# Transposing the attention output and the normalised rows of the last two chunks by DMA from SBUF instead of TensorE

## The chip, the cores and the metric

The kernel runs on one core of a Trainium2 chip. The metric is device microseconds of one execution, lower is better. Engines are named as in the profile: PE (TensorE), PEld (its weight loads), DVE (VectorE), ACT (ScalarE), POOL (GpSimd) and SP, the sync engine, whose queue issues all the DMAs of the part studied here (160 to 330 us), one after the other in program order. The record sorts runs into fast and slow ones; all runs quoted were in the fast state.

## The reference

It computes one transformer block forward and all its gradients, for 2048 tokens of width 640 in bfloat16: pre-norm linear attention (32 heads of width 20), then a gated MLP with 1728 hidden units. Only the forward pass between attention and MLP matters here.

```python
o = num / den                                   # linear attention, per head
h = x + o.reshape(B, S, D) @ wo                 # projection of the attention output
hn = layernorm(h)                               # "normalised rows"
gate, up = hn @ w1, hn @ w3                     # MLP, first matmuls
h2 = h + (silu(gate) * up) @ w2
```

In this kernel's matmuls the dimension that is summed over lies on the partitions, so `o` and `hn`, which are made with tokens on partitions, are transposed before `@ wo` and `@ w1`. Its PE transposes end in PSUM, where its matmul results go, and ScalarE copies them to SBUF (0.69 to 0.72 us for the five of a tile in the stretch used below).

## The kernel before

The 2048 tokens are four chunks of 512, each of four tiles of 128 tokens. While the MLP of chunk c runs in 14 steps (`fc`), the attention output, projection and norm of chunk c+1 are squeezed in between as "side" work. Position 0 lies between the gate and the up matmuls of a step, position 1 behind the step. Cuts are marked with `...`.

```python
def f2_o(t):                                   # DVE: attention output of tile t
    ...
    dma(out=o_v[:, t, :], in_=o_t[:])          # store, needed by the backward pass
    oT[t] = o_t

def f2_ot(t):                                  # PE transposes + ACT copy
    tr = ps.tile([P, DT, P], BF16, name="tr", bufs=1)
    for c in range(DT):                        # DT = 5 blocks of 128x128
        T.transpose(tr[:, c, :], oT[t][:, c * P:(c + 1) * P], ident[:])
    oT[t] = pf.tile([P, DT, P], BF16, name="oT", bufs=2)
    A.copy(out=oT[t][:], in_=tr[:])

def f2_at(t, tag="nd"):                        # projection with wo, PE waits for oT
    ...
def f2_hn(t):                                  # DVE: normalised rows, then their store
    ...
def f2_ht(t):                                  # the same five transposes for hn -> hnT
    ...

for i in range(TPC):                           # TPC = 4 tiles; (step, position, what)
    for k, pos, f in ((3 * i, 0, f2_ndo), (3 * i + 1, 1, f2_ot), (3 * i + 2, 1, f2_at), (3 * i + 3, 0, f2_hn),
                      (3 * i + 4, 0, f2_ht)):
        side[pos].setdefault(k, []).append((f, i))
```

Each MLP step also ends with three stores on SP (`hh_d`, and `gg_d` twice), which wait for DVE (one `hh_d` goes out at 231.57 us, DVE having finished its `hhT` at 231.54).

Of the kernel before, what the change touches and what calls it, by code (L numbers as in the profile page):

```python
# [8 lines left out]
P = 128  # L9
# [16 lines left out]
HD = D // 2  # L26
NG = 27
NB, NBLK = 288, 6


def _heads(lo, hi, g):
# [31 lines left out]
def kernel(  # L63
# [280 lines left out]
        oT[t] = o_t  # L344

    def f2_ot(t):
        tr = ps.tile([P, DT, P], BF16, name="tr", bufs=1)
        for c in range(DT):
            T.transpose(tr[:, c, :], oT[t][:, c * P:(c + 1) * P], ident[:])
        oT[t] = pf.tile([P, DT, P], BF16, name="oT", bufs=2)  # L350
        A.copy(out=oT[t][:], in_=tr[:])
# [36 lines left out]
    def f2_ht(t):  # L388
        c, i = divmod(t, TPC)
        if i == 0:  # L390
            hnT[c] = pf.tile([P, DT, W], BF16, name="hnT", bufs=2)
        tr = ps.tile([P, DT, P], BF16, name="tr", bufs=1)
        for d in range(DT):
            T.transpose(tr[:, d, :], hn[t][:, d * P:(d + 1) * P], ident[:])
        A.copy(out=hnT[c][:, :, i * P:(i + 1) * P], in_=tr[:])  # L395
# [81 lines left out]
    w2 = U1.tile([P, FT, D], BF16, name="w2", tag="D")  # L477
    V.memset(w2[64:, FT - 1, :], 0.0)

    side = ({}, {})  # L480
    for i in range(TPC):
        for k, pos, f in ((3 * i, 0, f2_ndo), (3 * i + 1, 1, f2_ot), (3 * i + 2, 1, f2_at), (3 * i + 3, 0, f2_hn),
                          (3 * i + 4, 0, f2_ht)):
            side[pos].setdefault(k, []).append((f, i))

    for c in range(SC):
        hhT[c] = pa.tile([P, FT, W], BF16, name="hhT", bufs=2)
        o2 = o2_steps(c - 1) if c > 0 else None

        def run_side(pos, fc):  # L490
            if c + 1 < SC:
                for f, i in sorted(side[pos].get(fc, ()), key=lambda x: x[1]):
                    f((c + 1) * TPC + i)

        for fc in range(FT):
            mlp(c, fc, lambda: run_side(0, fc))
            if o2:
                next(o2)
            run_side(1, fc)
            if fc == 1 and c == 0:  # L500
                dma(out=w2[:, 0:FT - 1, :], in_=B_w2[0:(FT - 1) * P, :].rearrange("(c p) n -> p c n", p=P))
                dma(out=w2[0:FL, FT - 1, :], in_=B_w2[(FT - 1) * P:F, :])
            if fc == 3 and c + 1 < SC:
                load_g2T(c + 1)
            if c == SC - 1 and fc == 0:
                g2 = U1.tile([P, ST, D], BF16, name="g2", tag="Q")
                for i in range(SC):
                    dma(out=g2[:, i * TPC:(i + 1) * TPC, :], in_=goS[:, i * TPC:(i + 1) * TPC, :])
            if c == SC - 1 and fc == 4:
                woT = U1.tile([P, DT, D], BF16, name="woT", tag="W6")  # L510
                dmaT(out=woT[:], in_=A_wo[:, :])
# [75 lines left out]
    def h1b(n):  # L587
        return ps.tile([P, n, P], BF16, name="h1b", tag="h1", bufs=2)
# [63 lines left out]
    def b_ln(acc, t):  # L652
        ln_rest[t] = ln_bwd(acc, t, hnb[t][:], ln2, g_h[:, t, :], g2[:, t, :], br)

    def b_gT(t):
        tr = h1b(DT)
        for c in range(DT):
            T.transpose(tr[:, c, :], g_h[:, t, c * P:(c + 1) * P], ident[:])
        ghT[t] = br.tile([P, DT, P], BF16, name="ghT", bufs=2)
        A.copy(out=ghT[t][:], in_=tr[:])  # L660
# [5 lines left out]
    def b_go(t):  # L666
        gnd[t] = gnd_s[t % 2]
        gv = gnd[t][:, 0:C].rearrange("p (h e) -> p h e", e=DA)
        prod = br.tile([P, H, DH], BF16, name="prod")
        gd = br.tile([P, H], F32, name="gd", bufs=2)  # L670
        for j in range(2):
            go = h1()
            hs = slice(j * 16, (j + 1) * 16)
            for c in range(DT):
                T.matmul(go[:, 0:HD], lhsT=ghT[t][:, c, :], rhs=woT[:, c, j * HD:(j + 1) * HD], start=(c == 0),  # L675
                         stop=(c == DT - 1))
            V.tensor_tensor(out=gv[:, hs, 0:DH], in0=go[:, 0:HD].rearrange("p (h d) -> p h d", d=DH),
                            in1=rden[:, t, hs].unsqueeze(2).to_broadcast([P, 16, DH]), op=ALU.mult)
        V.tensor_tensor(out=prod[:], in0=gv[:, :, 0:DH], in1=o_sb[:, t, :].rearrange("p (h d) -> p h d", d=DH),
                        op=ALU.mult)  # L680
        V.reduce_sum(out=gd[:], in_=prod[:], axis=AX.X)
        V.tensor_scalar(out=gv[:, :, DH], in0=gd[:], scalar1=-1.0, scalar2=None, op0=ALU.mult)

    def b_gndT(t):
        tr = h1b(CT)
        for cc in range(CT):
            T.transpose(tr[:, cc, :], gnd[t][:, cc * P:(cc + 1) * P], ident[:])  # L687
        gndT[t] = br.tile([P, CT, P], BF16, name="gndT", bufs=2)
        A.copy(out=gndT[t][:], in_=tr[:])

    def b_gkv(t):
        for m, (a, b) in enumerate(M_H):
            bank, off = KV_SLOT[m]
            T.matmul(gkv[:, bank, off:off + M_W[m]], lhsT=pqb[t][:, m * P:(m + 1) * P],
                     rhs=gnd[t][:, a * DA:b * DA], start=(t == 0 and off == 0), stop=(t == ST - 1),
                     skip_group_check=True)
# [33 lines left out]
    for t in range(ST + 3):  # L730
        g = b_ghn(t) if t < ST else wog

        def part():
            next(g, None)

        u, w = t - 2, t - 3
        if t + 2 < ST:
            b_load(t + 2)
        if 0 <= t - 1 < ST:
            b_load_q(t - 1)  # L740
        if t % 2 == 0 and 2 <= t <= ST - 2 and t // 2 + 1 < ST // 2:
            load_gg(t // 2 + 1)
        if 0 <= u < ST:
            b_gT(u)
        if t == ST:
            ln_rest.pop(t - 1)()
        part()
        if w >= 0:
            b_gndT(w)
            b_gkv(w)  # L750
        part()
        if 0 <= u < ST:
            b_go(u)
        part()
        if t - 1 in ln_rest and t < ST:
            ln_rest.pop(t - 1)()
        part()
        if w >= 0:
            b_gpq(w)
        part()  # L760
        part()
        if t == ST:
            xnN = U1.tile([P, ST, D], BF16, name="xnN", tag="Q")
            for i in range(SC):
                dma(out=xnN[:, i * TPC:(i + 1) * TPC, :], in_=xS[:, i * TPC:(i + 1) * TPC, :])
        if t > ST:
            for i in range(8):
                j = (t - ST - 1) * 8 + i
                ln1.norm(xnN[:, j, :], xnN[:, j, :], j)
# [100 lines left out]
    def load_block(i):  # L870
        if i < len(blocks):
            base, _, f0 = blocks[i]
            gb[i] = ex.tile([P, ST, NB], BF16, name="gb", bufs=3)
            dmaT(out=gb[i][:], in_=gg_d[base + f0:base + f0 + NB, :])

    for i in range(SC):
        dma(out=hnN[:, i * TPC:(i + 1) * TPC, :], in_=hn_v[:, i * TPC:(i + 1) * TPC, :])
    load_block(0)
    load_block(1)
    gT = {}  # L880

    def e_T(t, k):
        if k == 0:
            gT[t] = ex.tile([P, 15, P], BF16, name="gT", bufs=2)
        tr = ps.tile([P, DT, P], BF16, name="trq", bufs=2)
        for c in range(DT):
            T.transpose(tr[:, c, :], gqkv[k][:, t, c * P:(c + 1) * P], ident[:])  # L887
        if k == 1:
            V.tensor_copy(out=gT[t][:, k * DT:(k + 1) * DT, :], in_=tr[:])
        else:  # L890
            A.copy(out=gT[t][:, k * DT:(k + 1) * DT, :], in_=tr[:])

    def e_gxn(t):
        acc = ps.tile([P, 2, 512], F32, name="gxn", tag="gxn", bufs=2)
        for j in range(2):
            for k in range(15):
                T.matmul(acc[:, j, 0:HD], lhsT=gT[t][:, k, :], rhs=wqT[:, k, j * HD:(j + 1) * HD],  # L897
                         start=(k == 0), stop=(k == 14))
                if j * 15 + k in (7, 15, 23) and t + 1 < ST:
                    e_T(t + 1, (j * 15 + k) // 8)  # L900
        gx = ex.tile([P, D], BF16, name="gx", bufs=2)
        ln_bwd(acc, t, xnN[:, t, :], ln1, gx[:], g_h[:, t, :], ex)()
        A.dma_start(out=out1S[:, t, :], in_=gx[:])
# [5 lines left out]
    for k in range(3):  # L909
        next(jobs)  # L910
        next(jobs)
        e_T(0, k)
    for t in range(ST):
        next(jobs, None)
        e_gxn(t)
    for _ in jobs:
        pass

# [2 lines left out]
    ps = pool("pfp", space=PSUM)  # L921
    njob = 8
    for i, (_, out, f0) in enumerate(blocks):
        load_block(i + 2)
        for m in range(DT):
            grad_job(hnN, m, lambda t: gb[i][:, t, :], NB, out[:, m, f0:f0 + NB])
    ps.release()
# [35 lines left out]
```

## Time and profile before

| | before |
|---|---|
| time, median of 3 | 919.74 us (919.29 to 919.98) |
| PE busy | 96% of the span |
| PE busy, 165 to 305 us | 139.2 of 140 us |
| DVE, ACT busy, same stretch | 114.6 and 85.8 us |

How to read it: PE is busy 99% of this stretch and the list of its waits is empty there, so I take PE as what sets the pace. The lines themselves stand in the prediction below.

To compare kernels I use one **stretch**: from the start of the first group of output matmuls (`o<-w,hhT`) that runs between the MLP steps of chunk 1 to the first that runs between those of chunk 3. It holds all sixteen groups of transposes that the change removes. In the kernel before, its two ends are these lines of PE's timeline (start, duration, engine, line, operation, out<-in, shapes, count):

```profile
168.34 1.25 PE L448 MATMUL o<-w,hhT 128*128 128x320 bf16 x8
...
307.58 1.25 PE L448 MATMUL o<-w,hhT 128*128 128x320 bf16 x8
```

307.58 - 168.34 = 139.24 us. (The expectations for the first eight runs count the stretch from and to other marks, which makes it 135.99 us before.)

### The profile page before, as it was taken

Reading aid. Unit: us, or ns where it says so; the run is one execution under the profiler, and the core shown is the slowest. Engines: PE = TensorE matmul, PEld = TensorE weight load, DVE = VectorE, ACT = ScalarE, POOL = GpSimd, SP = SyncE. Lnnn points to the kernel's source line nnn. Section 1 sums busy time; section 2 is a strip of 40 time slices with the busy share of each in tenths; the row PEclk is TensorE's granted clock in tenths of the full one; section 3 lists DMA queues with packets and bytes.
Section 4 is the critical chain, followed back from the end, with each engine's and each line's share of the span. In section 5 each row is a group of like instructions: output and inputs, shape, how many; then the busy total and the mean of one; then the engine's idle time right before and its main releaser. Section 6 shows DMA issues by size and latency. Waiting matters only on the chain.

```text
span 917.3 us, 16861 instructions
## 1 busy us (share of the span) xinstructions
PE 883.4 (96%) x6729; PEld 611.5 (67%) x6757; DVE 449.0 (49%) x1146; ACT 388.7 (42%) x722; POOL 22.5 (2%) x42
## 2 busy tenths in 40 slices
PE   5999899999999999899999999999899999999998
PEld 3777554555555555677677777777677777777776
DVE  6776688888888677200145655555323443400000
ACT  3556777665565665011123223223334545422211
POOL 4000000000000000000000000000000000000000
PEclk9999999999999999999999999999999999999999
DMA  9678583353343552999444555148996011066861
GB/s 297 188 246 258 147 240 119 99 141 108 99 136 115 176 168 93 230 224 265 133 134 125 153 163 144 37 165 174 219 275 153 33 40 38 28 153 150 178 149 37
DMA packets 272447, 138.33 MB, mean 151 GB/s; under 512 B 173808, under 2 KB 271088, under 8 KB 272368
## 3 DMA queue, kind: packets, MB, share of 16 engines
q1 hardware_dynamic: 253856, 124.05, 51.8%
q10 hardware_dynamic: 18512, 13.20, 4.6%
q8 instruction: 53, 0.87, 0.4%
q14 instruction: 26, 0.21, 0.1%
HBM read 45.20 MB, written 50.02 MB: 104 GB/s over the span
## 4 chain that ended last, share of the span: by engine, by line
PE 82%; DVE 2%; DMA 2%; ACT 2%; issue 1%; ACTq 0%; DVEq 0%
PE job L796 20%; PE mm L400 19%; PE ghn L625 13%; PE gxn L897 7%; PE gw L559 7%; PE o L448 5%; PE h L675 2%; PE at L361 2%; PE gwo L716 2%; DMA hb<-hh_d 2%; PE trq L887 1%; DMA vaT<-va_d 1%; PE dkv L702 1%; PE h L702 1%; PE h1b L687 1%
## 5 line engine op out<-in xcount | busy, mean ns | idle before, releaser
L400 PE MATMUL mm<-hnT,w 128*128 128x512 bf16 x546 | 132.7, 379 | 1.7 <-ACT hnT L395 1.0
L796 PE MATMUL job<-gb,hnN 128*128 128x288 bf16 x960 | 117.8, 286 | 0.0
L796 PEld LDWEIGHTS <-hnN 128*128 128x128 bf16 x960 | 93.9, 98 | 23.7
L625 PEld LDWEIGHTS <-ggb 128*128 128x128 bf16 x864 | 82.4, 98 | 30.2 <-issue 0.5
L400 PEld LDWEIGHTS <-w 128*128 128x128 bf16 x560 | 53.8, 98 | 61.3 <-issue 1.1
L800 ACT CAST obs<-job 128x288 bf16<-128x288 f32 (+1 forms) x90 | 36.8, 409 | 132.9 <-PE job L796 88.0
L897 PE MATMUL gxn<-wqT,gT 128*128 128x320 bf16 x480 | 74.8, 299 | 0.0
L400 PE MATMUL mm<-g2T,w2T 128*128 128x512 bf16 x266 | 68.3, 379 | 0.8
L448 PE MATMUL o<-w,hhT 128*128 128x320 bf16 x448 | 67.9, 299 | 1.0 <-DVE h L453 1.0
L625 PE MATMUL ghn<-w13a,ggb 128*128 128x320 bf16 x448 | 67.8, 299 | 0.0
L559 PE MATMUL gw<-g,hb 128*128 128x320 bf16 (+1 forms) x448 | 61.1, 299 | 1.3 <-DMA hb<-hh_d 1.3
L219 PE MATMUL big<-wqkv,pqT 128*128 128x320 bf16 x400 | 59.6, 305 | 2.7 <-DVE kvacc L258 1.0
L625 PE MATMUL ghn<-w13b,ggb 128*128 128x320 bf16 x416 | 61.2, 299 | 0.0
L448 PEld LDWEIGHTS <-hhT 128*128 128x128 bf16 x448 | 43.8, 98 | 24.9 <-issue 1.2
L219 PEld LDWEIGHTS <-pqT 128*128 128x128 bf16 x480 | 46.4, 99 | 20.8 <-DVE kvacc L258 1.3
L412 ACT CAST ghh<-mm 128x512 bf16<-128x512 f32 x56 | 32.9, 588 | 63.3 <-issue 39.3
L796 PEld LDWEIGHTS <-xnN 128*128 128x128 bf16 x480 | 47.2, 99 | 18.5
L559 PEld LDWEIGHTS <-hb 128*128 128x128 bf16 (+1 forms) x448 | 44.1, 99 | 18.4 <-DMA hb<-hh_d 1.7
L897 PEld LDWEIGHTS <-gT 128*128 128x128 bf16 x480 | 45.1, 98 | 14.8
L636 ACT ACTIVATE gs<-ghn 128x640 bf16<-128x640 f32 x16 | 11.3, 705 | 95.8 <-PE ghn L625 95.8
L648 ACT ACTIVATE y<-wb,s,ln_rs 128x640 bf16<-128x640 f32 x32 | 29.4, 920 | 40.9 <-DVE wb L644 40.9
L420 ACT ACTIVATE sig<-mm 128x512 bf16<-128x512 f32 x56 | 33.4, 597 | 24.8 <-PE mm L400 24.1
(136 smaller groups left out, 1212.0 us busy)
## 6 DMA issues: line engine op xcount, KB each, us to landing
ggb<-gg_d SPq DMA_DIRECT2D x8, 1728.0 KB, 9.5
hh_d<-hhT SPq DMA_DIRECT2D x52, 128.0 KB, 1.8
gg_d<-gate SPq DMA_DIRECT2D x52, 128.0 KB, 1.9
gg_d<-sig SPq DMA_DIRECT2D x52, 128.0 KB, 1.8
out_dram<-obs ACTq DMA_DIRECT2D x60, 72.0 KB, 2.7
w<-in_B_w_dram SPq DMA_DIRECT2D x4, 864.0 KB, 5.5
va_d<-va SPq DMA_DIRECT2D x4, 768.0 KB, 6.5
out_dram<-gw2o ACTq DMA_DIRECT2D x18, 160.0 KB, 4.7
```

What stands on the lines that cost most here:

```text
L219: T.matmul(acc, lhsT=pqT[:, c, t * P:(t + 1) * P], rhs=wqkv[:, c, n0:n0 + HD], start=(c == 0), stop=(c == DT - 1))
L361: T.matmul(at[:, 0:HD], lhsT=oT[t][:, c, :], rhs=wo[:, c, j * HD:(j + 1) * HD], start=(c == 0 and not on_pe), stop=(c == DT - 1))
L400: T.matmul(acc[:], lhsT=w[:, c, fc * P:(fc + 1) * P], rhs=rhs[:, c, :], start=(c == 0), stop=(c == DT - 1))
L412: A.copy(out=ghh[fc][:], in_=acc[:])
L420: A.activation(sig[:], gp[:], AF.Sigmoid)
L448: T.matmul(o2["ps"][:, 0:HD], lhsT=hhT[c][:, fc, i * P:(i + 1) * P], rhs=w2[:, fc, j * HD:(j + 1) * HD], start=(fc == 0), stop=(fc == FT - 1))
L559: T.matmul(acc[:n, j, 0:HD], lhsT=hb[b][:, t, i * P:i * P + n], rhs=g2[:, t, j * HD:(j + 1) * HD], start=(t == 0), stop=(t == ST - 1))
L625: T.matmul(acc[:, j, 0:HD], lhsT=ggb[t // 2][:, k, lo:lo + P], rhs=rhs[:, j * HD:(j + 1) * HD], start=(k == 0), stop=(k == NG - 1))
L648: A.activation(out=y[:], in_=wb[:], func=AF.Identity, bias=s[:, 3:4], scale=st.rs[:, t:t + 1])
L796: T.matmul(acc[:, 0:n], lhsT=lhs[:, t, m * P:(m + 1) * P], rhs=rhs(t), start=(t == 0), stop=(t == ST - 1))
L800: A.copy(out=ob, in_=acc[:, 0:n])
L897: T.matmul(acc[:, j, 0:HD], lhsT=gT[t][:, k, :], rhs=wqT[:, k, j * HD:(j + 1) * HD], start=(k == 0), stop=(k == 14))
```

## The change

Its intent is to take work off PE, the bound: the transposes of chunks 2 and 3 (tiles 8 to 15) become DMA transposes, SBUF to SBUF, on the SP queue, and the ACT copies out of PSUM vanish. As a DMA takes time to land (2.6 us in the median here, see below), the attention output's transpose is moved one step earlier, to just behind the step that makes it, and that of the normalised rows from inside a step to just behind the step before. Two further parts of the diff (TR_B, TR_E) are switched off, and are cut here, as is their code.

```diff
+TR_A, TR_B, TR_E = 1, 0, 0
     def f2_ot(t):
+        if TR_A and t >= 2 * TPC:
+            o_t, oT[t] = oT[t], pf.tile([P, DT, P], BF16, name="oT", bufs=2)
+            dmaT(out=oT[t][:], in_=o_t[:])
+            return
     def f2_ht(t):
+        if TR_A and t >= 2 * TPC:
+            dmaT(out=hnT[c][:, :, i * P:(i + 1) * P], in_=hn[t][:])
+            return
-    (3 * i + 1, 1, f2_ot), ... (3 * i + 4, 0, f2_ht)
+    (3 * i + 1 - tr, 1, f2_ot), ... (3 * i + 4 - tr, tr, f2_ht)
+    sides = [sides(0), sides(TR_A), sides(TR_A)]
```

More of the change, by code (lines that the diff above doesn't have):

```diff
@@ L478, with sides @@
     V.memset(w2[64:, FT - 1, :], 0.0)
-    side = ({}, {})
-    for i in range(TPC):
-        for k, pos, f in ((3 * i, 0, f2_ndo), (3 * i + 1, 1, f2_ot), (3 * i + 2, 1, f2_at), (3 * i + 3, 0, f2_hn),
-                          (3 * i + 4, 0, f2_ht)):
-            side[pos].setdefault(k, []).append((f, i))
+    def sides(tr):
+        side = ({}, {})
+        for i in range(TPC):
+            for k, pos, f in ((3 * i, 0, f2_ndo), (3 * i + 1 - tr, 1, f2_ot), (3 * i + 2, 1, f2_at),
+                              (3 * i + 3, 0, f2_hn), (3 * i + 4 - tr, tr, f2_ht)):
+                side[pos].setdefault(k, []).append((f, i))
+        return side
+    sides = [sides(0), sides(TR_A), sides(TR_A)]
     for c in range(SC):
@@ L491, in run_side @@
             if c + 1 < SC:
-                for f, i in sorted(side[pos].get(fc, ()), key=lambda x: x[1]):
+                for f, i in sorted(sides[c][pos].get(fc, ()), key=lambda x: x[1]):
                     f((c + 1) * TPC + i)
@@ L653, in b_ln, with by_dma @@
         ln_rest[t] = ln_bwd(acc, t, hnb[t][:], ln2, g_h[:, t, :], g2[:, t, :], br)
+    def by_dma(t):
+        return TR_B and t < ST - 2
     def b_gT(t):
+        if by_dma(t):
+            ghT[t] = br.tile([P, DT, P], BF16, name="ghT", bufs=2)
+            dmaT(out=ghT[t][:], in_=g_h[:, t, :])
+            return
         tr = h1b(DT)
@@ L684, in b_gndT @@
     def b_gndT(t):
+        if by_dma(t):
+            gndT[t] = br.tile([P, CT, P], BF16, name="gndT", bufs=2)
+            dmaT(out=gndT[t][:], in_=gnd[t][:])
+            return
         tr = h1b(CT)
@@ L742 @@
             load_gg(t // 2 + 1)
-        if 0 <= u < ST:
+        if 0 <= u < ST and not by_dma(u):
             b_gT(u)
@@ L748 @@
         if w >= 0:
-            b_gndT(w)
-            b_gkv(w)
+            if not by_dma(w):
+                b_gndT(w)
+            if not TR_B:
+                b_gkv(w)
         part()
-        if 0 <= u < ST:
+        if 0 <= u < ST and not TR_B:
             b_go(u)
@@ L756 @@
             ln_rest.pop(t - 1)()
+            if by_dma(t - 1):
+                b_gT(t - 1)
+        if w >= 0 and TR_B:
+            b_gkv(w)
         part()
-        if w >= 0:
+        if 0 <= u < ST and TR_B:
+            b_go(u)
+        if w >= 0 and not TR_B:
             b_gpq(w)
@@ L761 @@
         part()
+        if w >= 0 and TR_B:
+            b_gpq(w)
+        if 0 <= u < ST and by_dma(u):
+            b_gndT(u)
         if t == ST:
@@ L874, in load_block, with load_hnN @@
             dmaT(out=gb[i][:], in_=gg_d[base + f0:base + f0 + NB, :])
-    for i in range(SC):
-        dma(out=hnN[:, i * TPC:(i + 1) * TPC, :], in_=hn_v[:, i * TPC:(i + 1) * TPC, :])
-    load_block(0)
-    load_block(1)
+    def load_hnN():
+        for i in range(SC):
+            dma(out=hnN[:, i * TPC:(i + 1) * TPC, :], in_=hn_v[:, i * TPC:(i + 1) * TPC, :])
+    if not TR_E:
+        load_hnN()
+        load_block(0)
+        load_block(1)
     gT = {}
@@ L883, in e_T @@
         if k == 0:
-            gT[t] = ex.tile([P, 15, P], BF16, name="gT", bufs=2)
+            gT[t] = ex.tile([P, 15, P], BF16, name="gT", bufs=3 if TR_E else 2)
+        if TR_E:
+            dmaT(out=gT[t][:, k * DT:(k + 1) * DT, :], in_=gqkv[k][:, t, :])
+            return
         tr = ps.tile([P, DT, P], BF16, name="trq", bufs=2)
@@ L898, in e_gxn @@
                          start=(k == 0), stop=(k == 14))
-                if j * 15 + k in (7, 15, 23) and t + 1 < ST:
+                if j * 15 + k in (7, 15, 23) and t + 1 < ST and not TR_E:
                     e_T(t + 1, (j * 15 + k) // 8)
@@ L912 @@
         e_T(0, k)
+    if TR_E:
+        for t in (1, 2):
+            for k in range(3):
+                e_T(t, k)
+        load_hnN()
     for t in range(ST):
@@ L915 @@
         e_gxn(t)
+        if TR_E:
+            for k in range(3):
+                if t + 3 < ST:
+                    e_T(t + 3, k)
+            if t in (5, 9, 13):
+                load_block((t - 5) // 4)
     for _ in jobs:
@@ L923 @@
     for i, (_, out, f0) in enumerate(blocks):
-        load_block(i + 2)
+        load_block(i + 2 + TR_E)
         for m in range(DT):
```

## The prediction

> **What bounds the kernel now.** I read the page's table of engines first, then the stretches that the change touches, then the chain of waits.
>
> ```profile
> PE 883.4 (96%) x6729; PEld 611.5 (67%) x6757; DVE 449.0 (49%) x1146; ACT 388.7 (42%) x722; POOL 22.5 (2%) x42
> 165.00:235.00 70.00, 69.58 (x421) 39.20 (x428) 57.61 (x157) 43.49 (x81) 2.20 (x4) 1.00 0.38 116
> 235.00:305.00 70.00, 69.63 (x421) 39.19 (x428) 57.02 (x156) 42.34 (x78) 2.19 (x4) 1.00 0.37 115
> 165.00:235.00 70.00, 3.54 (x40) 6.38 (x9) 1.00 0.38 116
> 235.00:305.00 70.00, 3.54 (x40) 5.66 (x8) 1.00 0.37 115
> ```
>
> The first row says that TensorE (PE) is busy 96% of the span. The next two are the stretches in which the gated MLP of chunks 1 and 2 runs; squeezed between its steps are the attention output and the normalisation of the next chunk, 2 and then 3. There PE is busy 69.6 of 70 us, VectorE 57, ScalarE 43, at full clock, with the DMA engines 38% busy. The last two rows are the same stretches for the transposes' PSUM tile alone: 40 PE transposes and eight or nine ScalarE copies in each (a ninth belongs to the chunk before). So in these 140 us PE sets the time and nearly everything else lies beside it. The chain of waits agrees: between 160 and 365 us it is PE matmuls almost without a break, up to 368.72 us, where a load of the hidden activations begins (14 us). That load starts when this stretch ends, so what is won or lost here moves the end one for one.
>
> [...] the trace shows 219 ns as the duration of one PE transpose, but five of them push the next matmul back by only 0.28 us. [...] 640 KB land in 5.4 us, 121 GB/s, so I use the durations of the trace.
>
> **What is removed.** For 8 row tiles of 128 tokens (the last two chunks), two groups of five transposes each: 16 groups, 80 PE transposes with 80 weight loads, and 16 ScalarE copies. The instruction order of the changed kernel confirms it: 160 PE rows less, 16 ScalarE rows less, 16 rows more on the sync engine's DMA queue (SP). What a group costs PE is read from the start of the next thing, not from its own 0.44 us, which contains pipelined tail:
>
> ```profile
> 299.74 1.24 PE L400 MATMUL mm<-g2T,w2T 128*128 128x512 bf16 x4
> 300.82 1.24 PE L400 MATMUL mm<-hnT,w 128*128 128x512 bf16 x5
> 301.90 0.44 PE L394 MATMUL tr<-ident,hn 128*128 128x128 bf16 x5
> 302.18 1.24 PE L400 MATMUL mm<-hnT,w 128*128 128x512 bf16 x5
> 303.26 1.25 PE L448 MATMUL o<-w,hhT 128*128 128x320 bf16 x8
> 304.35 1.24 PE L400 MATMUL mm<-g2T,w2T 128*128 128x512 bf16 x5
> 305.42 2.32 PE L400 MATMUL mm<-hnT,w 128*128 128x512 bf16 x10
> ```
>
> 302.18 - 301.90 = 0.28 us. Sixteen groups: 16 x 0.28 = 4.5 us, all of it on the path. The ScalarE copies are 16 x 0.7 = 11 us, but ScalarE is 62% busy here and mostly waits for PE, so they are worth nothing. The few waits of PE for the transposes' single PSUM buffer (2.7 us in all) lie before 165 us, in chunk 0, whose transposes stay. So 4.5 us, 0.5% of the time, is the ceiling: 915.2 us.
>
> **What is added.** Sixteen DMA transposes, 128x640 from SBUF to SBUF, in the in-order SP queue, each placed behind the stores of its MLP step. There is no record of one this small. The nearest:
>
> ```profile
> L190 SPq DMA_TRANSPOSE g2T<-in_grad_out_dram x4: 2830/3011/3581, 32.2 to 259.1; - x4
> DMA to landing us min/median/max: 4.8/5.4/6.1
> L874 SPq DMA_TRANSPOSE gb<-gg_d x12: 4727/4844/11370, 676.2 to 884.9; - x12
> DMA to landing us min/median/max: 7.4/7.7/14.8
> ```
>
> The first is 512x640 (20 blocks of 128x128), the second 288x2048 (36 blocks). From the shortest times the queue is held (4.73 - 2.83)/16 = 0.12 us a block, and five blocks cost 2.83 - 15 x 0.12 = about 1.0 us; with the 2.69 us of the pqT transposes as base it is about 0.8. Landing follows the end of the issue by 4.8 - 2.7 = 2.1 us at best. Estimate: **0.8 us of queue, 2.9 us from issue to landing**, with a DRAM source; I choose the same for SBUF.
>
> **Is it early enough?** Two kinds of consumer. The output of attention (oT) is needed by the projection two MLP steps later. In the first tile of each chunk it is issued 5 us ahead: hidden. In the other three it goes out behind the stores of its step and behind another tile's hnT transpose. Take the middle one of the second chunk: the SP queue is free at about 274.7 us (the store of h at 274.25 takes 0.38), hnT goes first, 0.8 plus a 0.1 gap, then oT lands 2.9 later, at 278.5. The projection starts at 278.73; two transpose groups between the step and it vanish, so PE will want it at 278.73 - 0.56 = 278.2. A stall of 0.35 us. The same sum gives 0.35 for its twin in the first chunk, and about 0 to 0.05 for the other four. The second kind is the last normalised tile of a chunk (hnT), which the next chunk's first gate matmul needs: its stores are issued until 302.61 + 0.33, it lands at 303.0 + 2.9 = 305.9, and PE wants it at 305.42 - 0.28 = 305.1, a stall of 0.8 us. One chunk earlier a store took 1.79 us instead of 0.35 and held the queue: 0.25 us without that accident, 1.9 with it. Sum of stalls 1.8 to 3.5 us; I take 2.3.
>
> **Net: 4.5 removed, 2.3 given back, 2.2 us gained: 917.5 us.**
>
> **Rivals.** (a) **All is hidden.** If a small transpose from SBUF lands in about 2.2 us, only the last tile of each chunk is near its deadline, and the full 4.5 us show: 915.2. For it: ordinary 160 KB stores land in 1.8 us. Against: even the shortest transposes on record land 2 us after issue. (b) **The wait takes the place of the work.** Eight consumers (six oT, two hnT) sit within 1 us of their deadline. Every 1 us that a transpose takes beyond my estimate costs up to 8 us, and for the six oT it counts nearly twice, since two transposes stand in a row. With 1.1 us of queue and 3.4 of landing the stalls are near 7 us and the kernel comes out at about 922. For it: [...] some transposes on record take over 1 us more than the shortest. (c) **The SP queue becomes the bound.** It gains 16 x 0.8 = 13 us over 140, and has about 1.1 to 1.5 us of issues per MLP step of 4.3 us, so it has room; the stores it delays feed triple-buffered tiles. I give this little. (d) **DMA bandwidth.** 16 x 160 KB is 2.6 MB beside engines that are 38% busy: nothing.
>
> **Range and chances.** The floor is the ceiling of the gain less the noise of 0.3 us: 914.9. The top is rival (b): 922.5. To be slower by 2% (18.4 us) the transposes would have to land about 2 us later than estimated at all eight places: 3%. Faster by 2% would need four times what is removed: 0.5%. The rest is within 2%.
>
> **What would show it.** The stretch's PE rows lose 80 transposes, and the gap from one projection to the next shrinks by 0.56 us if nothing waits. New PE waits, if I am right, stand at the first gate matmul of chunks 2 and 3 (released by a DMA into hnT) and, smaller, at the projections (a DMA into oT), 2 to 3 us in sum, none anywhere else. The new transposes should hold the queue 0.8 us and land in 2.9. The prediction is wrong if these two durations are off by half a microsecond or more, upward above all, or if the transposes disturb the stores around them.

Passages that no trace or run here shows are cut from it; of rival (b)'s two grounds that leaves the second, the spread of the transposes on record. No term of its sum is among them: 4.5 us removed, 2.3 given back, 2.2 gained. For its 0.7 us of ScalarE a group, the trace has 692 to 722 ns. Of ScalarE's 54.2 us without work between 165 and 305 us, 28.2 ended with a PE matmul.

## The result, and the profile after

Ratios here and below are the mean time of one kernel's fast runs over that of the other's in the same rounds, so they are not quite the ratio of the medians. In the first sitting the change took 918.67 us against 919.86, ratio 0.9982 (0.9965 to 0.9999). A sitting is one set of runs on one chip. Two later sittings of the same kernel gave 916.31 against 919.79 (0.9964, 0.9952 to 0.9977) and 916.74 against 920.38 (0.9961, 0.9948 to 0.9973). So it is a small gain, 0.2 to 0.4%, well within the 2% that the record counts as the same.

The same two stretches as in the prediction, first for all engines (columns: stretch, length, then busy us of PE, PEld, DVE, ACT, POOL with counts, TensorE clock granted as a share of full speed, mean busy share of the 16 DMA engines, GB/s), in the changed kernel:

```profile
165.00:235.00 70.00, 69.38 (x394) 37.68 (x400) 59.18 (x161) 39.67 (x76) 2.20 (x4) 1.00 0.47 137
235.00:305.00 70.00, 68.43 (x384) 36.81 (x388) 58.14 (x158) 37.13 (x71) 2.20 (x4) 1.00 0.49 135
```

PE is no longer quite full: 137.8 of 140 us where it was 139.2. Something waits. The list of PE's waits between 160 and 330 us (waiter, releaser, total us, times, longest), which is empty of DMAs in the kernel before, says what:

```profile
PE at L366 <- DMA oT<-o_t: 0.7, 2, 0.5
PE mm L408 <- DMA hnT<-hn: 0.4, 1, 0.4
PE mm L408 <- issue: 0.4, 1, 0.4
```

The third line is the same wait at the start of chunk 3, whose releaser the profile did not match; e5 below shows both chunk starts under the DMA's name. In PE's timeline the two stand here (the bracket is PE's idle time just before, and what ended it):

```profile
236.35 1.24 PE L408 MATMUL mm<-hnT,w 128*128 128x512 bf16 x5 [0.43 <-DMA hnT<-hn]
305.21 2.32 PE L408 MATMUL mm<-hnT,w 128*128 128x512 bf16 x10 [0.40 <-issue]
```

The durations of the new instructions (min/median/max ns, then from issue to landing in us):

```profile
L350 SPq DMA_TRANSPOSE oT<-o_t x8: 1221/1228/1268, 174.9 to 290.3; - x8
DMA to landing us min/median/max: 2.6/2.6/3.0
L398 SPq DMA_TRANSPOSE hnT<-hn x8: 1209/1211/1219, 191.0 to 302.5; - x8
DMA to landing us min/median/max: 2.6/2.6/3.7
```

Each holds the SP queue for 1.21 to 1.27 us, and in the median it lands 2.6 us after its issue begins (160 KB, 63 GB/s; the 640 KB transposes from DRAM, g2T, landed in 5.4 us in the kernel before, 121 GB/s). The place of the longest wait, the third tile of chunk 3, first in SP's timeline and then in PE's:

```profile
273.71 0.33 SPq L445 DMA_DIRECT2D gg_d<-sig  x1
274.14 0.38 SPq L463 DMA_DIRECT2D out_dram<-h  x1
274.57 1.21 SPq L398 DMA_TRANSPOSE hnT<-hn  x1
275.87 1.23 SPq L350 DMA_TRANSPOSE oT<-o_t  x1
277.19 0.53 SPq L440 DMA_DIRECT2D hh_d<-hhT  x1
```

```profile
277.14 1.25 PE L456 MATMUL o<-w,hhT 128*128 128x320 bf16 x8
278.87 1.53 PE L366 MATMUL at<-wo,oT 128*128 128x320 bf16 x10 [0.49 <-DMA oT<-o_t]
280.24 1.24 PE L408 MATMUL mm<-g2T,w2T 128*128 128x512 bf16 x4
```

The transpose that PE wants next (oT) stands behind one that nobody wants for another 30 us (hnT of the tile before, first read by the gate matmul at 305.21), and that stands behind the step's stores. It is issued at 275.87, and the projection starts 3.0 us later. Part of this wait is not the order: at this one place the two transposes landed 3.0 us (oT) and 3.7 us (hnT) after issue instead of 2.6, and much the same in the two later profiles. Why is not tested. Note also that the bracket (0.49 us) is not the whole cost: it counts from the end of the pipelined tail of the matmuls before. The output matmuls usually give way to the next group 1.09 us after they start, at 278.23; PE starts 0.64 us after that.

The two ends of the stretch in the changed kernel:

```profile
170.29 1.25 PE L456 MATMUL o<-w,hhT 128*128 128x320 bf16 x8
...
307.37 1.25 PE L456 MATMUL o<-w,hhT 128*128 128x320 bf16 x8
```

Stretch of the changed kernel: 307.37 - 170.29 = 137.08 us, **2.16 us less** than before; 137.18 and 136.99 in the two later profiles.

### The profile page after: what moved, and what is told of

Same layout as the page of the kernel before. It is cut to its first block, busy times and chain, and to the rows that moved or that the text cites. A ratio compares the mean times of both kernels' runs of the same rounds, so it can differ in the third digit from the quotient of the medians.

```text
span 916.9 us, 16717 instructions
## 1 busy us (share of the span) xinstructions
PE 882.1 (96%) x6650; PEld 607.9 (66%) x6677; DVE 449.7 (49%) x1146; ACT 377.9 (41%) x706; POOL 22.5 (2%) x42
## 4 chain that ended last, share of the span: by engine, by line
PE 77%; DMA 6%; DVE 4%; ACT 2%; issue 1%; SPq 0%; POOL 0%; ACTq 0%; DVEq 0%
PE job L830 19%; PE mm L408 16%; PE ghn L636 13%; PE gxn L938 7%; PE gw L570 7%; PE o L456 4%; PE h L693 2%; DMA vaT<-va_d 2%; PE gwo L738 2%; PE at L366 2%; PE trq L928 1%; DMA hb<-hh_d 1%; DMA oT<-o_t 1%; PE h L724 1%; PE h1b L709 1%
## 5 line engine op out<-in xcount | busy, mean ns | idle before, releaser
L570 PE MATMUL gw<-g,hb 128*128 128x320 bf16 (+1 forms) x448 | 61.1, 299 | 0.2 <-DMA hb<-hh_d 0.2
```

The costliest lines, as they stand in the source:

```text
L570: T.matmul(acc[:n, j, 0:HD], lhsT=hb[b][:, t, i * P:i * P + n], rhs=g2[:, t, j * HD:(j + 1) * HD], start=(t == 0), stop=(t == ST - 1))
```

## The experiments

All results in one table. "Stretch" is read from the start times in each profile; "against before" is its difference from 139.24; "expected" is the difference that the text implies.

| run | stretch us | against before | expected | time, median us | time ratio (95%) |
|---|---|---|---|---|---|
| e1_again, the change | 137.18 | -2.06 | -2.2 | 916.31 | 0.9964 (0.9952 to 0.9977) |
| e2_early | 134.80 | -4.44 | -4.5 | 915.17 | 0.9948 (0.9935 to 0.9962) |
| e3_ot_only | 137.43 | -1.81 | -2.2 | 917.69 | 0.9983 (0.9969 to 0.9997) |
| e4_hn_only | 138.15 | -1.09 | -1.1 | 918.72 | 0.9987 (0.9975 to 1.0000) |
| e5_swap | 136.08 | -3.16 | -3.6 | 915.55 | 0.9947 (0.9933 to 0.9961) |
| e6_late | 152.43 | +13.19 | +10 to +28 | 933.20 | 1.0149 (1.0126 to 1.0172) |
| e7_twice | 143.74 | +4.50 | +4.5 | 923.47 | 1.0027 (1.0014 to 1.0041) |
| e8_early3 | 134.80 | -4.44 | -4.5 | 912.54 | 0.9919 (0.9905 to 0.9932) |
| e9_after, the change | 136.99 | -2.25 | -2.1 | 916.74 | 0.9961 (0.9948 to 0.9973) |
| e10_early | 134.78 | -4.46 | -4.4 | 914.19 | 0.9936 (0.9924 to 0.9949) |
| e11_split | 134.77 | -4.47 | -4.4 | 911.03 | 0.9900 (0.9884 to 0.9915) |
| e12_control, before | 139.27 | +0.03 | 0 | 920.45 | 0.9998 (0.9986 to 1.0011) |

Kernels e1 to e4, e5 to e8, and e9 to e11 ran together on one chip each. All outputs are right.

### e7_twice: what a group of transposes costs PE

The kernel before, with every group of tiles 8 to 15 issued twice into the same PSUM tile.

```diff
-        for c in range(DT):
+        for c in list(range(DT)) * (2 if t >= 2 * TPC else 1):
             T.transpose(tr[:, c, :], oT[t][:, c * P:(c + 1) * P], ident[:])
```

> The kernel before with each of the 16 groups of PE transposes issued twice into the same PSUM tile (the second overwrites the first with the same values, the result is right). It measures the cost of a group by itself. Theory: 16 x 0.28 = 4.5 us more, stretch 140.5, ratio 1.0049. Rival (a group hides partly beside other work, and the change gained less because it removed less): 1 to 3 us more.

A doubled group in PE's timeline of e7:

```profile
246.96 0.72 PE L349 MATMUL tr<-ident,o_t 128*128 128x128 bf16 x10
247.52 1.24 PE L400 MATMUL mm<-g2T,w2T 128*128 128x512 bf16 x4
```

Ten transposes push the next matmul back by 0.56 us, though the record of a single one lasts 219 ns in the kernel before. The stretch grew by 4.50 us for 80 more transposes, 0.28 us a group, 56 ns each. The first term of the prediction is measured by itself and holds. The time grew by only about 2.7 us; that belongs to the last part of this section.

### e2_early and e10_early: is the rest queue position?

Both transposes are issued directly behind the DVE instruction that makes their data, ahead of the store of the same tile and of the step's three stores. The old places become empty.

```diff
     def f2_o(t):
+        if t >= 2 * TPC:
+            oT[t] = pf.tile([P, DT, P], BF16, name="oT", bufs=2)
+            dmaT(out=oT[t][:], in_=o_t[:])
         dma(out=o_v[:, t, :], in_=o_t[:])
     def f2_hn(t):
+        if t >= 2 * TPC:
+            ...
+            dmaT(out=hnT[c][:, :, i * P:(i + 1) * P], in_=hn[t][:])
         dma(out=hn_v[:, t, :], in_=hn[t][:])
```

> Both DMA transposes put into the queue directly after the VectorE instruction that makes their data, ahead of the step's stores. Theory (the stalls are queue position, 2.6 us in six places): each lands 3 to 4 us earlier, no PE wait for oT or hnT is left, the stretch is 135.99 - 4.5 = 131.5 us, the kernel 915.2, ratio 0.995. Rival (the transposes cost PE something else, contention or slower stores): the waits vanish from the trace but the stretch stays near 133.8.

> Both transposes issued right behind their producer, again, to compare with e11 on the same chip. Stretch 134.8, 4.4 us below before, ratio 0.9950.

The same tile as above now goes out long before the step's stores, in SP's timeline of e2_early, and its projection follows the output matmuls without a bracket, in PE's:

```profile
269.05 1.21 SPq L346 DMA_TRANSPOSE oT<-o_t  x1
270.31 0.57 SPq L349 DMA_DIRECT2D o_d<-o_t  x1
270.98 0.38 SPq L446 DMA_DIRECT2D hh_d<-hhT  x1
271.45 0.41 SPq L448 DMA_DIRECT2D gg_d<-gate  x1
271.95 0.40 SPq L451 DMA_DIRECT2D gg_d<-sig  x1
272.44 0.39 SPq L469 DMA_DIRECT2D out_dram<-h  x1
```

```profile
274.69 1.25 PE L462 MATMUL o<-w,hhT 128*128 128x320 bf16 x8
275.77 1.52 PE L368 MATMUL at<-wo,oT 128*128 128x320 bf16 x10
```

And PE is busy 140.00 of the 140 us from 165 on:

```profile
165.00:235.00 70.00, 70.00 (x399) 37.97 (x398) 59.54 (x162) 39.55 (x75) 2.19 (x4) 1.00 0.51 137
235.00:305.00 70.00, 70.00 (x402) 38.31 (x401) 58.21 (x159) 39.21 (x74) 2.19 (x4) 1.00 0.51 137
```

All 4.5 us of the removed work now show in the stretch (-4.44, -4.46). So the rival, some contention that costs PE time without a wait, is out: the same sixteen transposes, at a DMA share that is no lower (0.51), are free when they are issued early. The waits of the change cost 137.08 - 134.80 = 2.28 us.

### e3_ot_only and e4_hn_only: each half alone

In one the normalised rows stay on PE, in the other the attention output does, each at its old place.

```diff
 e3:  f2_ht:  if TR_A and t >= 2 * TPC   ->   if 0 ...   and (3 * i + 4, 0, f2_ht)
 e4:  f2_ot:  if TR_A and t >= 2 * TPC   ->   if 0 ...   and (3 * i + 1, 1, f2_ot)
```

> Only the attention output by DMA, the normalised rows by PE as before. Theory: no hnT transpose stands in front of an oT one in the queue, so oT lands 1.3 us earlier and none of its four stalls (1.5 us) is left; 8 groups x 0.28 = 2.2 us gained, stretch 133.8, ratio 0.9976. Rival (a DMA transpose is late by itself): stalls of 0.2 to 0.6 us at the projections stay, stretch near 135.

> Only the normalised rows by DMA. Theory: 2.2 us removed, the two waits at the start of chunks 2 and 3 stay (0.59 and 0.56 us), 1.1 us gained, stretch 134.9, ratio 0.9988, and no wait elsewhere.

e4 is as expected: 2.24 us removed, two waits at the chunk starts, 1.09 us left. In e3 three of the four stalls are gone. One of about 0.4 us stays, in front of the projection of the second tile of chunk 2: its oT was issued at 188.98 us, the 640 KB g2T load went out directly behind it at 190.29, and it landed 4.5 us after issue (the median of the eight is 2.6). So "the order alone" was slightly too simple: the bulk load issued just behind this transpose may have delayed its landing. PE waited in one of the two such places of that run, and the landing was late in neither of the two in the first profile of the change (2.6 and 2.7 us); no run tests it by itself.

### e5_swap: only the order

In steps that issue both, oT goes ahead of hnT.

```diff
-    sorted(sides[c][pos].get(fc, ()), key=lambda x: x[1])
+    sorted(sides[c][pos].get(fc, ()), key=lambda x: (c > 0 and x[0] is f2_ht, x[1]))
```

> As the change, but in each step that issues both, the oT transpose goes into the queue ahead of the hnT one. Theory: oT lands 1.3 us earlier, its four stalls (0.22, 0.36, 0.25, 0.64 us) vanish, the two at the chunk starts (0.6 each) stay: stretch 133.83 - 1.5 = 132.4. Rival (the projection waits because of landing time, not of the order): stretch 133.8.

PE's waits from 160 us on, in e5:

```profile
PE mm L408 <- DMA hnT<-hn: 0.9, 2, 0.4
```

No wait for oT is listed; both chunk starts still wait for hnT. The stretch is 1.0 us below the change. I had expected 1.5: I had taken the stalls at the projections as 1.47 us by counting each from the 1.09 us of an output group. Comparing steps with those of e2_early instead (0.13, 0.27, 0.17 and 0.56) gives 1.1, because a gap of 0.09 us behind the `nd` matmuls of such steps stands in e2_early too and is swallowed by the stall in the change. The remaining tenth is a stall too small for the list: at the third tile of chunk 3, where oT took 3.6 us to land, the projection still starts 1.26 us after its output group instead of 1.08.

### e6_late: the same transposes with one step less lead

> As the change, but the oT transposes are issued one MLP step (4.3 us of PE) later, where the PE transposes stood. Theory (a DMA transpose is worth it only with lead): the first tile of each chunk stalls 1 to 1.5 us, the second, behind the g2T load, about 6, the others 3.5 to 4.5; about 30 us in sum over two chunks minus what stands now, so 12 to 30 us slower than the change, ratio to before 1.01 to 1.03. Rival (PE would absorb it): within 3 us of the change.

```diff
-    (3 * i + 1 - tr, 1, f2_ot)
+    (3 * i + 1, 1, f2_ot)
```

PE's waits for oT went from 0.7 us to 14.2 us:

```profile
PE at L366 <- DMA oT<-o_t: 14.2, 8, 3.1
```

The stretch is 15.3 us longer than with the change and the time 1.5% above before: the same DMA transposes, placed where the PE transposes stood, turn a gain into a loss. The sum is in the expected band, but its parts are not: at the second tile of each chunk I expected about 6 us and the waits are 3.1, and at four tiles (the last two of each chunk) I expected 3.5 to 4.5 us and the waits cost 1.2 to 1.8. Two things shorten the latter: no hnT transpose stands in front any more (1.3 us), and the step's stores, behind which oT goes, leave earlier in a step whose DVE has no attention work (before, at these tiles, the last of the three stores ends 4.0 to 4.5 us after the start of the step's output matmuls, against 5.7 in the steps that have it).

One wait shows a second cost. After 3.10 us without work, PE ran slowly for a while, in PE's timeline and then in a four-microsecond stretch, where the clock stands before the last two numbers:

```profile
198.84 2.78 PE L366 MATMUL at<-wo,oT 128*128 128x320 bf16 x10 [3.10 <-DMA oT<-o_t]
201.42 1.71 PE L408 MATMUL mm<-g2T,w2T 128*128 128x512 bf16 x5
```

```profile
199.00:203.00 4.00, 4.00 (x16) 1.98 (x15) 1.79 (x5) 0.00 (x0) 0.00 (x0) 0.58 0.23 73
```

The ten projection matmuls take 2.78 us instead of 1.52, at a granted clock of 0.58. The length of the gap alone does not decide it here: a gap of 3.07 us in the same run was followed by full speed (1.53 us), and in e12_control a gap of only 1.95 us was followed by slow matmuls (37 in 6.87 us, where the kernel before has 54 in 7.51; the longest record lasts 474 ns, against 323).

### e8_early3 and e11_split: going further

e8 is e2 with chunk 1 by DMA too (`t >= TPC`), 24 groups in all.

> As e2_early, and chunk 1 (its tiles are prepared beside chunk 0 of the MLP) by DMA too: 24 groups. Theory: 8 more groups of 0.28 us off PE, and the PE waits for the single PSUM tile of the transposes that stand in that stretch (1.1 us) go too: 2.2 to 3.3 us below e2_early, ratio 0.992. Rival: in chunk 0 a step lasts only 3.2 us of PE and the attention output of the next tile is asked for sooner, so that waits for the DMA eat 1 us or more of it.

Within the stretch nothing changes. Chunk 1 is prepared before it, beside chunk 0 of the MLP: from the first gate matmul of chunk 0 to the first output matmul of chunk 1 the kernel before takes 60.06 us, and e8 takes 59.97, nothing for 2.2 us removed. The reason is one line of PE's timeline:

```profile
128.04 0.30 PE L366 MATMUL at<-x_sb,ident 128*128 128x320 bf16 x1
131.57 1.07 PE L368 MATMUL at<-wo,oT 128*128 128x320 bf16 x5 [3.23 <-DMA oT<-o_t]
```

One oT took 6.2 us to land (the hnT just before it 8.2), and PE waited 3.23 us and then ran at a clock of 0.57 (mean of 132 to 136 us). The 2.1 MB load of w2 was issued 7.6 us before that transpose; in the kernel before, the same load lands 8.8 us after its issue. The time of e8, 912.54 us, is 2.6 us below that of e2_early, the number expected, but it was measured on another chip, and the profile shows no such gain. e11 cuts that load in four and puts the pieces between the transposes:

```diff
-            if fc == 1 and c == 0:
-                dma(out=w2[:, 0:FT - 1, :], in_=B_w2[0:(FT - 1) * P, :]...)
+            if fc in (1, 4, 7, 10) and c == 0:
+                c0, c1 = {1: (0, 4), 4: (4, 7), 7: (7, 10), 10: (10, 13)}[fc]
+                dma(out=w2[:, c0:c1, :], in_=B_w2[c0 * P:c1 * P, :]...)
```

> e8_early3 with the 2.1 MB load of w2 in chunk 0 cut in four and put between the transposes of chunk 0. In e8 the projection of the tile whose oT transpose ran beside that load waited 3.2 us (landing 6.2 us instead of 2.6), and chunk 0, from its first gate matmul to the first output matmul of chunk 1, took 59.97 us against 60.06 before: 8 groups were taken off PE there for nothing. Theory (contention with the bulk load): that wait goes, chunk 0 takes 56.7 to 57.5 us, the kernel comes out 2.5 to 3.3 us below e10. Rival (the small transposes land late in chunk 0 whatever the load, or the smaller loads come in the way four times): waits of over 1 us for oT stay.

PE's only wait for oT in e11:

```profile
PE at L368 <- DMA oT<-o_t: 1.0, 1, 1.0
```

Chunk 0 took 56.22 us, 3.8 less than before and half a microsecond better than expected, and the kernel came out 3.2 us below e10 on the same chip (911.03 and 914.19). The 3.8 us are more than the 2.2 us of the eight groups, because PE's three waits for the PSUM tile of the transposes, 2.7 us in chunk 0 before (not 1.1, as I had written for e8), are gone too, while one wait of 1.0 us for oT is left. So the bulk load was what had eaten the gain. e11 is the fastest version found: ratio 0.9900 to the kernel before, against 0.9961 for the change in the same sitting.

### e1_again, e9_after and e12_control: how much of the time is the change?

> The changed kernel unchanged, to get its ratio with more rounds. Stretch = from the first w2T matmul of the second MLP step of chunk 1 to the first gate matmul of chunk 3; it was 135.99 us before and 133.83 in the first profile of the changed kernel, 2.2 us less, while the profiled spans differ by only 0.4. Theory (start-up noise): the part before 107 us is the same program and lost its 2 us by chance, so the stretch comes out at 133.8 again and the whole is 2 us below before, ratio 0.998, with some runs further off. Rival (the change costs something elsewhere): the stretch is 133.8 and every profile is about 2 us late before the stretch begins, ratio 0.999.

> The changed kernel a third time, beside e10 and e11 on one chip: the first sitting gave ratio 0.9982, the second 0.9964, though the stretch was 137.1 and 137.2 us (from the first output matmul of chunk 1 to that of chunk 3; 139.24 before) in both. Theory: the change is worth 2.1 us and the rest is scatter of the parts that it does not touch: stretch 137.1, ratio 0.9977 within 0.0015. Rival (something outside the stretch is gained): ratio at or below 0.9964 again.

> The kernel before, run as if it were a changed one, against itself. In the traces the changed kernel gains 2.1 us in the stretch that the change touches, but three sittings gave 1.2, 3.5 and 3.6 us in the time; the kernel with the PE transposes doubled loses 4.5 us in the stretch and only 2.7 in the time. Theory (the comparison, not the kernel: scatter and the place of a kernel in a sitting): this copy comes out up to 1.5 us below itself, ratio 0.9985 to 1.0, and the part after the stretch, 609.7 us in the first profile of before, is 607 to 609.5 here as in the other profiles. Rival (the kernels with other code really gain 1 to 2 us outside the stretch): ratio 1.0 within 0.0005 and 609.7 us again.

The stretch repeats to 0.2 us (137.08, 137.18, 136.99), while the time gained 1.2, 3.5 and 3.6 us by the medians (1.7, 3.3 and 3.6 by the ratios). So the ratios of e1 (0.998 expected) and e9 (0.9977 within 0.0015; the rival had 0.9964 or less) were missed. The control shows no bias of the comparison (0.9998), so my theory of e12, that a copy might come out 1.5 us below itself, falls. The part after the stretch took 613.1 us in its profile, which neither the theory nor the rival had; that profile is of its slowest run (923.67 us). Outside the stretch, the fourteen profiles agree to a tenth of a microsecond in most parts, and differ in three, e12 in a fourth: the start-up (79.3 to 81.8 us to the first late q matmul), the part from the first `job` matmul to the first `gxn` matmul near 690 us, in which PE waits for the loads pkT and vaT (59.5 to 61.5 us) and the part from the end of the stretch to the first weight-gradient matmul; in e12 also the weight-gradient matmuls behind it (62.75 us against 61.1), which hold the slow matmuls mentioned under e6. In the part before the first weight-gradient matmul PE waits for the first transposed load of the hidden activations. Before and, below it, e9_after (the last line of each is cut off):

```profile
367.90 13.47 PE L448 MATMUL o<-w,hhT 128*128 128x320 bf16 x98 [0.95 <-DVE h L453]
...
382.72 7.51 PE L559 MATMUL gw<-g,hb 128*128 128x320 bf16 x54 [1.35 <-DMA hb<-hh_d]
```

```profile
366.11 13.47 PE L456 MATMUL o<-w,hhT 128*128 128x320 bf16 x98 [0.95 <-DVE h L461]
379.55 5.74 PE L570 MATMUL gw<-g,hb 128*128 128x320 bf16 x41
```

This part took 75.14 and 75.75 us in the two profiles of the kernel before and 75.48 in e3, but 73.6 to 74.1 in all other eleven, e7 among them, which has the DMAs of the kernel before. That is 1.0 to 2.1 us in a wait that the change does not touch. It fits part of the record: -2.1 in the stretch and about -1.4 here make the 3.5 us of two sittings; e7, +4.5 and -1.5 to -2.1, makes its 2.7; e3, which keeps the wait, gained 2.1 us in the time for 1.8 in the stretch. It does not fit the first sitting and e4, which lack the wait in their profiles (3.3 and 2.6 us by this sum) and gained only 1.2 and 1.1 us in the time, nor e8, which gained 7.5 us by its ratio where the sum gives 6.0. There is one profile of each kernel, or two or three, so I can't say why that load lands earlier in the others, and leave it open.

## Why the prediction was right, point by point

- **What bounds.** Right: taking work off PE shortened the stretch by that work once nothing waited (4.44 of 4.5 us, e2), and adding work lengthened it by that (4.50 us, e7).
- **Removed, 16 x 0.28 = 4.5 us.** Right: 4.50 us by e7, 4.44 to 4.46 by e2 and e10.
- **The ACT copies are worth nothing.** Fits: with them gone e2 gained no more than PE's share (4.44 of 4.5 us).
- **The cost of a DMA transpose, "0.8 us of queue, 2.9 us from issue to landing".** Both terms were off, in opposite directions: 1.21 us of queue and 2.6 us to landing. For oT, which stands behind an hnT, the sum counts (0.8 + 0.1 + 2.9 = 3.8 foretold, 1.3 + 2.6 = 3.9 measured), so the errors cancelled, by luck. By the prediction's own test (half a microsecond) both stand, the queue term with 0.41 us barely. The queue term came from a per-block slope of transposes with a DRAM source, continued to five blocks and an SBUF source; I chose that, and it missed by half.
- **Stalls "1.8 to 3.5 us; I take 2.3".** 2.28 us in sum, in the places named; that the sum is met so closely is luck. By place, foretold and measured against e2's steps: middle tiles 0.35 and 0.35, measured 0.27 and 0.56 (where the landing was late); the other four 0 to 0.05, measured 0.13, 0.17 and twice 0; the last hnT of chunk 3 0.8, measured 0.56. The last hnT of chunk 2 was foretold as 0.25 without the accident of the 1.79 us store, measured 0.59 without it; part of the 2.3 stood for that accident, which did not happen. That term was mis-sized: I took the accident off the queue in full, though the store behind it waits for DVE until 232.8 us anyway, so the transpose could not go out at 232.7.
- **Rivals.** (a), all hidden, is what e2 makes of it. (b) is the right mechanism: e6 shows how steep it is (PE's waits for oT went from 0.7 to 14.2 us). (c), SP as the bound, did not come about (in e2 PE is busy all 140 us), though its occupation per transpose was larger than I had it. (d) was right for the two chunks (DMA share 0.38 to 0.47 and 0.49), but too quick as a rule: in e8 a bulk load did delay a small transpose (6.2 us to land; 3.9 at most for oT with the load cut in four, e11), and perhaps in e3.
- **"What is won or lost here moves the end one for one."** The weakest step. The wait for the hidden activations just behind the stretch varied by 1.0 to 2.1 us between kernels, as large as the effect, so the time is 1.2 to 3.6 us better where the stretch says 2.1, and what makes up the difference is not shown. The 917.5 us foretold lies between the sittings' 918.67 and 916.31.

## What to carry to other kernels

In this kernel a group of transposes moved from PE to DMA gained what it cost PE in the stream (start of the next matmul minus its own start, 0.28 us by e7), and gave back what it landed after its consumer's turn (2.28 us over the sixteen in the change, nothing that shows in e2, and in e6 so much that the stretch came out 13.19 us longer than before). So place it by landing time: issue it right behind its producer, ahead of stores that nobody waits for (worth the 2.28 us in e2), and order what is wanted first in front (1.0 us in e5). Look at which bulk load is in flight there before you do the same in the next stage (in e8 one transpose landed in 6.2 us instead of 2.6, and PE waited 3.23). And judge an effect of a few microseconds by the stretch that it touches, in several profiles, because the rest of this kernel scattered as much (1.0 to 2.1 us in the wait behind the stretch alone).
